# Layer 2's narrow outputs in runs of plain fp32 products, and two layers taking turns by steps

## The chip, the cores and the metric

One NeuronCore of a Trainium2 chip runs the whole kernel. The metric is device time in microseconds (us) of one execution, lower being better. TensorE (PE; its weight loads have rows of their own, PEld) does the matrix products, ScalarE (ACT) and VectorE (DVE) the elementwise work, GpSimd (POOL) a little at the start, and SyncE (SP) issues the DMAs.

## The reference

A causal convolution with seven softmax taps per head runs over (2, 4096, 192) tokens, and its output goes through two gated layers, each 192 → 2048 → 192:

```
x = einsum('hk,bskhg->bshg', softmax(weight), x_unf)     # 8192 tokens x 192
h = x @ w_in1                                            # 192 -> 2048
g = where(h >= 1, h, where(h <= -1, 0, (h + 1)**2 / 4))
x = g @ w_out1                                           # 2048 -> 192
h = x @ w_in2
g = h / (1 + exp(-1.702 * h))
out = g @ w_out2
```

All inputs and outputs are fp32.

## The kernel before

Tokens lie along the free axis, in 16 blocks of 512. The 192 channels are 128 ("a") and 64 ("b"); each layer's 2048 hidden channels are 16 units of 128. A **phase** is one layer of one block. A **step** takes two units: PE makes the hidden values of units u and u+1 in two PSUM banks (`pair`; there are two such pairs, used in turn), ACT and DVE turn them into gated values `a`, and two steps later (`LAG` = 4 units) PE multiplies these by the second weights into two accumulator banks: `acc_a` for the first 128 outputs and `acc_b` for the last 64. There are 256 steps, 8 in a phase. From step 32 on the phases of layer 1 and layer 2 follow one another, 8 whole steps each: layer 1 of block i, then layer 2 of block i-1.

To keep fp32 accuracy in the rounded type fp32r, every operand is split into a high and a low part (`ghi`, `glo` for the gated values, `wh`, `wl` for weights), and three of the four partial products are made. For the 64 narrow outputs the high and low weights lie side by side as 128 columns (`wb`), multiplied by `ghi` and by `glo`: two products, whose two halves of 64 rows of `acc_b` are added when the phase ends.

A product with 128 contraction rows is cut into two of 64 rows, one on the lower and one on the upper half of the PE array, and `couples` (L437) issues them in turn, lower, upper, lower, upper: a **couple** is two such products side by side, usually for different banks. A step (`both`, L468) is 19 couples: 9 for the hidden values, 6 for `acc_a`, 4 for `acc_b`. When a bank has to be written by the other half than the last time, `couples` puts a pause before that product, in which PE's queue waits for a product that carries a signal (a set of numbers, `{6, 18, 37}`, says which of the step's 38 products do).

The gate of layer 1 (`gates`, L368) is: ACT `early` on both banks (L347), ACT `square` on each (L352), DVE `bound` on each (L356, which still reads the hidden bank), ACT `high` (L360) and DVE `low` (L364) on each. Layer 2 needs ACT `early` (L349), `high` and DVE `low` on each bank. So a pair of banks is free for PE once both `bound`s (layer 1) or both `early`s (layer 2) are done. `finish` turns the accumulators into layer 2's input or the output. The convolution's taps (L192, DVE) for coming blocks are spread over the steps by `conv_at`. In the first two steps (`first_only`, L458) hidden values alone are made, in three stretches with a pause ahead of the last; before them the first block's convolution runs on PE in plain fp32 (`conv_by_quarters`, L238, and `conv_by_sides`, L227: 128 rows by 64 columns, two such products side by side in the array's two column halves, three on each side).

Of the kernel before, what the change touches and what calls it, by code (L numbers as in the profile page):

```python
# [10 lines left out]
U32 = mybir.dt.uint32  # L11
# [9 lines left out]
def kernel(  # L21
# [37 lines left out]
    stage = ctx.enter_context(tc.tile_pool(name="stage", bufs=2))  # L59
    xt_p = ctx.enter_context(tc.tile_pool(name="xt", bufs=2))  # L60
    cv_p = ctx.enter_context(tc.tile_pool(name="cv", bufs=2))
    xs_p = ctx.enter_context(tc.tile_pool(name="xs", bufs=4))
    a_p = ctx.enter_context(tc.tile_pool(name="a", bufs=2))
    g_p = ctx.enter_context(tc.tile_pool(name="g", bufs=LAG))
    o_p = ctx.enter_context(tc.tile_pool(name="o", bufs=1))
    ps = ctx.enter_context(tc.tile_pool(name="ps", bufs=1, space=bass.MemoryType.PSUM))
# [43 lines left out]
    words = {1: w1, 2: w2}  # L110
    wt = {n: wpool.tile([P, NG, 2 * WC], F32R, name=f"wt{n}") for n in (1, 2)}
    halves_of = (slice(0, IN), slice(IN, WC))
    whole = slice(0, WC)

    def weight_tile():
        return stage.tile([P, WC, 2], U32, tag="raw", name="raw", bufs=3)

# [13 lines left out]
    def weight_tiles():  # L131
        a = stage.tile([P, WC], F32, tag="wa", name="wa", bufs=2)
        d = stage.tile([P, WC], U32, tag="wd", name="wd", bufs=3)
        return a, d

# [41 lines left out]

    def new_xs():
        return [xs_p.tile([P, T], F32R, tag=t, name=t) for t in ("xah", "xal", "xbh", "xbl")]

    def x_load(part, i, queue=None):

        t = xt_p.tile([P, T + 128], F32, tag=f"xt{part}", name="xt", bufs=2 - part)[:, 0 : PAD + T]
        (queue or nc.sync).dma_start(t, (xb if part else xa)[i])  # L184
        return t
# [89 lines left out]

    def conv_ops(j):

        ta, tb = xt[0, B * j], xt[1, j]
        ca = cv_p.tile([P, T], F32, tag="cva", name="cva")
        cb = cv_p.tile([P, T], F32, tag="cvb", name="cvb", bufs=1)  # L280
        x1[B * j] = new_xs()
        ops = conv_taps(0, ta, ca) + [lambda: put_a(B * j, ca)]
        ops += conv_taps(1, tb, cb) + [lambda: put_b(B * j, cb)]
        st = {}

        def begin():
            st["c"] = cv_p.tile([P, T], F32, tag="cva", name="cva")
            x1[B * j + 1] = new_xs()
            st["ops"] = conv_taps(0, xt[0, B * j + 1], st["c"])
            put_b(B * j + 1, cb)  # L290

        ops.append(begin)
        ops += [lambda: st["ops"].pop(0)() for _ in range(K)] + [lambda: put_a(B * j + 1, st["c"])]
        return ops


    phases = [(1, 0), (1, 1), (2, 0), (2, 1), (1, 2)]
    for i in range(3, NBLK):
        phases += [(1, i), (2, i - 1)]
# [11 lines left out]
    units += in_turn((2, 8), (3, 8), (2, 8), (3, 8))  # L311
    units += [(p, f) for p in range(4, len(phases)) for f in range(NF)]
    unit_at = {u: k for k, u in enumerate(units)}

    hid, act, halves, accs = {}, {}, {}, {}
    HID = 4
# [22 lines left out]
    def gate_ops(u):  # L339

        n, _ = phases[units[u][0]]
        h = hid.pop(u)
        a = a_p.tile([P, 2, T], F32, tag="a", name="a")

        def early(k=slice(0, 2)):
            if n == 1:
                nc.scalar.activation(a[:, k], h[:, k], AF.Relu, bias=0.5, scale=0.5)  # L347
            else:
                nc.scalar.activation(a[:, k], h[:, k], AF.Gelu_apprx_sigmoid)  # L349

        def square(k=slice(0, 2)):
            nc.scalar.activation(a[:, k], a[:, k], AF.Square)  # L352

        def bound(k):
            if n == 1:
                nc.vector.scalar_tensor_tensor(a[:, k], h[:, k], 1.0, a[:, k], op0=ALU.max, op1=ALU.min)  # L356

        def high(k):
            halves[u + k] = [g_p.tile([P, T], F32R, tag=t, name=t) for t in ("ghi", "glo")]
            nc.scalar.copy(halves[u + k][0], a[:, k])  # L360

        def low(k):
            hi, lo = halves[u + k]
            nc.vector.tensor_sub(lo, a[:, k], f32(hi))  # L364

        return early, square, bound, high, low

    def gates(u, conversions=()):  # L368
# [20 lines left out]
        else:  # L389
# [18 lines left out]

    def gemm2_whole(us):

        p = units[us[0]][0]
        acc_a, acc_b = accs[p]
        a, b = [], []
        for u in us:
            wh, wl, wb = out_w(u)
            hi, lo = halves.pop(u)
            a += [(acc_a, wl, hi), (acc_a, wh, hi), (acc_a, wh, lo)]
            b += [(acc_b, wb, hi), (acc_b, wb, lo)]
        closing = (b[-1], a[-1]) if us[-1] == len(units) - 1 else ()
        for x in b + a:  # L420
            nc.tensor.matmul(*x, start=False, stop=any(x is y for y in closing))  # L421

# [45 lines left out]
    def both(u, v):  # L468
# [16 lines left out]
        couples(low, up, banks, fresh, closing, {6, 18, 37})  # L485

    def finish_ops(p):
        i = phases[p][1]
        acc_a, acc_b = accs.pop(p)
        ah, al, bh, bl = x2[i] = new_xs()  # L490
        s = cv_p.tile([P, T], F32, tag="cva", name="s")
        other = slice(DB, P), slice(0, DB)
        return [
            lambda: nc.scalar.copy(s[other[1]], acc_b[other[0]]),
            lambda: nc.scalar.copy(s[other[0]], acc_b[other[1]]),
            lambda: nc.vector.tensor_add(s, acc_b, s),
            lambda: nc.scalar.copy(bh, s),
            lambda: nc.vector.tensor_sub(bl, s, f32(bh)),
            lambda: nc.scalar.copy(ah, acc_a),
            lambda: nc.vector.tensor_sub(al, acc_a, f32(ah)),  # L500
        ]

    def finish(p, step):
# [10 lines left out]
        else:  # L514
            acc_a, acc_b = accs.pop(p)
            o = o_p.tile([P, 2, T + 32], F32, tag="o", name="o")[:, :, 0:T]
            nc.scalar.copy(o[0:DB, 1], acc_b[DB:P])
# [6 lines left out]

            if p < len(phases) - 1:
                at(step + 2, rest)
            else:
                nc.vector.tensor_add(o[0:DB, 1], acc_b[0:DB], o[0:DB, 1])
# [47 lines left out]
    def conv_at(j):  # L576
        first, second = (unit_at[phases.index((1, B * j + k)), 0] for k in range(B))
        ops, begin = [], first - (20 if j == 1 else 22)
        at(begin - 8, lambda: fetch_x((0, B * j), (1, j), (0, B * j + 1)))
        at(begin, lambda: ops.extend(conv_ops(j)))  # L580
        for k in range(2 * (K + 1)):
            at(begin + k, lambda: ops.pop(0)())
        for k in range(K + 2):
            at(second - 16 + k, lambda: ops.pop(0)())

    with tc.manual_schedule():
        first, second = halves_of
        nc.sync.dma_start(taps, taps_in)  # L588
        fetch_x((0, 0), (1, 0))
        pair_x = o_p.tile([P, 2, T + 32], F32, tag="o", name="xt")[:, :, 0 : PAD + T]  # L590
        load_twice(pair_x, xa[1].rearrange("(j p) c -> j p c", j=2))
# [15 lines left out]
        for i in range(B):  # L607
            x1[i] = new_xs()
        ca = cv_p.tile([P, T], F32, tag="cva", name="cva")
        a0 = conv_taps(0, xt[0, 0], ca, exps)  # L610
        db = a_p.tile([P, 2, T], F32, tag="a", name="diag").rearrange("p k t -> p (k t)")
# [3 lines left out]
        da = [f32(t).rearrange("p (k c) -> p k c", c=H) for t in new_xs()[0:2]]  # L615
        da = [[d[:, m] for m in range(K // 2)] for d in da]
# [26 lines left out]
        for j in range(1, NBLK // B):  # L643
            conv_at(j)

        def of(ops, step):
# [30 lines left out]
        beside(1)  # L677
        for u in range(LAG, len(units) + LAG + 4, 2):
            v, step = u - LAG, u // 2
            if u < len(units):  # L680
                both(u, v)
# [5 lines left out]
            elif v < len(units):  # L687
                gemm2_whole((v, v + 1))
            beside(step)
            finish_if_last(v + 1, u + 1)  # L690

# [54 lines left out]
```

## Time and profile before

| | |
|---|---|
| median of 3 runs | 1125.14 us (1124.90 to 1125.28) |
| the profiled execution | 1124.4 us |
| its span, first to last instruction | 1122.6 us |
| PE busy | 1117.6 us, 100% |
| ACT busy | 830.1 us, 74% |
| DVE busy | 709.8 us, 63% |
| granted TensorE clock, mean | 1.00 |

The span is 1.8 us shorter than the profiled execution's time, and the median is 0.74 us above that. Busy time is a union over an engine's instructions. A matmul's row lasts 387 ns on average, but its successors on the same half start 227 ns apart, so times between starts, and not durations, tell what PE is doing.

### The profile page before, as it was taken

The page shows a single profiled execution, that of the slowest core. Times are in us where ns is not written, and L with a number is a line of the kernel's source. Part 1 is how long each engine was busy: PE and PEld are TensorE (multiplying, and loading weights), DVE is VectorE, ACT ScalarE, POOL GpSimd, SP SyncE. Part 2 cuts the span into 40 slices and gives each one's busy share as a digit, 9 for nine tenths or more (in the row PEclk, how much of TensorE's full clock was granted, in tenths as well). Part 3 has the DMA queues.
Part 4 walks back from the last instruction along what each step waited for, and adds up shares of the span by engine and source line. Part 5 has one row for each costly group of instructions (what it writes and reads, how often), then busy time and mean ns, then how long its engine had stood idle before and what let it go on. Part 6 is the DMA issues. An engine that isn't in the chain of part 4 may idle for free.

```text
span 1122.6 us, 23931 instructions
## 1 busy us (share of the span) xinstructions
PE 1117.6 (100%) x9788; PEld 1093.4 (97%) x9788; DVE 709.8 (63%) x1098; ACT 830.1 (74%) x1312; POOL 5.5 (0%) x14
## 2 busy tenths in 40 slices
PE   9999999999999999999999999999999999999998
PEld 5889999999999999999999999999999999999998
DVE  8997767765647557475665755657566575655432
ACT  8998678867767687776877768677686776867754
POOL 1000000000000000000000000000000000000000
PEclk9999999999999999999999999999999999999999
DMA  7442011000100001000010000100001000000000
GB/s 200 136 117 68 1 44 34 1 11 15 30 11 15 11 15 39 10 7 10 16 39 15 1 11 16 39 15 1 11 15 39 15 1 11 15 11 15 1 1 29
DMA packets 23900, 30.71 MB, mean 27 GB/s; under 512 B 3312, under 2 KB 15856, under 8 KB 23792
## 3 DMA queue, kind: packets, MB, share of 16 engines
q1 hardware_dynamic: 23648, 29.06, 9.2%
q8 instruction: 77, 1.26, 0.5%
q14 instruction: 31, 0.25, 0.1%
q10 hardware_dynamic: 144, 0.13, 0.0%
HBM read 19.22 MB, written 6.29 MB: 23 GB/s over the span
## 4 chain that ended last, share of the span: by engine, by line
PE 99%; DMA 0%; SPq 0%; ACT 0%; issue 0%
PE acc L446 51%; PE pair L446 47%; PE cb_ps L238 1%; PE acc L421 0%; DMA xt<-in_xb_dram 0%; PE ca_ps L227 0%; SPq L184 0%; SPq L588 0%; ACT o L531 0%; ACT o L533 0%
## 5 line engine op out<-in xcount | busy, mean ns | idle before, releaser
L446 PE MATMUL acc<-ghi,wt 64*128 64x512 f32 x3048 | 657.6, 387 | 0.0
L446 PE MATMUL acc<-glo,wt 64*128 64x512 f32 x2032 | 566.0, 387 | 0.0
L446 PEld LDWEIGHTS acc<-ghi,wt 64*128 64x128 f32 x3048 | 484.7, 184 | 3.5
L364 DVE TENSOR_TENSOR glo<-a,ghi 128x512 fp32r<-128x512 f32 x512 | 342.7, 690 | 224.5 <-ACT ghi L360 206.7
L446 PE MATMUL pair<-xah,wt 64*128 64x512 f32 x2048 | 429.8, 387 | 0.1
L360 ACT CAST ghi<-a 128x512 fp32r<-128x512 f32 x512 | 314.7, 622 | 44.2 <-DVE a L356 35.3
L446 PEld LDWEIGHTS acc<-glo,wt 64*128 64x128 f32 x2032 | 336.2, 184 | 3.5 <-DVE glo L364 1.0
L446 PE MATMUL pair<-xal,wt 64*128 64x512 f32 x1024 | 308.3, 387 | 0.0
L446 PEld LDWEIGHTS pair<-xah,wt 64*128 64x128 f32 x2048 | 302.5, 185 | 5.0 <-ACT xbh L251 1.6
L356 DVE SCALAR_TENSOR_TENSOR a<-pair,a 128x512 f32<-128x512 f32 x256 | 164.8, 685 | 162.9 <-ACT a L352 142.5
L349 ACT ACTIVATE a<-pair 128x512 f32<-128x512 f32 x256 | 152.2, 595 | 146.4 <-PE pair L446 146.4
L446 PE MATMUL pair<-xbh,wt 64*128 64x512 f32 x1024 | 260.3, 387 | 0.0
L446 PE MATMUL pair<-xbl,wt 64*128 64x512 f32 x512 | 197.2, 387 | 0.0
L446 PEld LDWEIGHTS pair<-xbh,wt 64*128 64x128 f32 x1024 | 186.3, 185 | 1.4
L347 ACT ACTIVATE a<-pair 128x1024 f32<-128x1024 f32 x128 | 131.4, 1026 | 63.7 <-PE pair L446 49.3
L446 PEld LDWEIGHTS pair<-xal,wt 64*128 64x128 f32 x1024 | 153.3, 184 | 1.6 <-DVE xal L254 0.2
L352 ACT ACTIVATE a<-a 128x512 f32<-128x512 f32 (+1 forms) x242 | 146.5, 650 | 4.1
L446 PEld LDWEIGHTS pair<-xbl,wt 64*128 64x128 f32 x512 | 94.1, 184 | 0.7
L192 DVE SCALAR_TENSOR_TENSOR cva<-xt,taps,cva 128x512 f32<-128x512 f32 x84 | 62.9, 749 | 1.5
L192 DVE SCALAR_TENSOR_TENSOR cvb<-xt,taps,cvb 128x512 f32<-128x512 f32 x42 | 31.5, 749 | 0.7
L79 ACT CAST xbh<-cvb 64x512 fp32r<-64x512 f32 x14 | 8.7, 618 | 10.1 <-DVE cvb L192 10.0
L155 DVE SCALAR_TENSOR_TENSOR wd<-wa,wd 128x768 uint32<-128x768 uint32 (+2 forms) x18 | 15.6, 866 | 0.7
(68 smaller groups left out, 249.3 us busy)
## 6 DMA issues: line engine op xcount, KB each, us to landing
raw<-in_w_dram SPq DMA_DIRECT2D x48, 128.0 KB, 2.3
xt<-in_xa_dram SPq DMA_DIRECT2D x17, 259.0 KB, 2.9
out_dram<-o SPq DMA_DIRECT2D x15, 256.0 KB, 2.0
raw<-in_w_dram SPq DMA_DIRECT2D x48, 64.0 KB, 2.3
raw<-in_w_dram SPq DMA_DIRECT2D x16, 192.0 KB, 2.5
out_dram<-o SPq DMA_DIRECT2D x17, 128.0 KB, 2.3
xt<-in_xb_dram SPq DMA_DIRECT2D x8, 259.0 KB, 3.0
xbh<-xbh SPq DMA_DIRECT2D x14, 128.0 KB, 2.2
```

The source lines that it names most:

```text
L79: nc.scalar.copy(hi, src)
L155: nc.vector.scalar_tensor_tensor(d(), a().bitcast(U32), 3, d(), op0=ALU.logical_shift_left, op1=ALU.bitwise_or)
L192: return lambda: nc.vector.scalar_tensor_tensor(c, x, w, c, op0=ALU.mult, op1=ALU.add)
L238: nc.tensor.matmul(c[o], d[k][r, r], t[r, k : k + T], start=k == 0, stop=k == K - 1)
L347: nc.scalar.activation(a[:, k], h[:, k], AF.Relu, bias=0.5, scale=0.5)
L349: nc.scalar.activation(a[:, k], h[:, k], AF.Gelu_apprx_sigmoid)
L352: nc.scalar.activation(a[:, k], a[:, k], AF.Square)
L356: nc.vector.scalar_tensor_tensor(a[:, k], h[:, k], 1.0, a[:, k], op0=ALU.max, op1=ALU.min)
L360: nc.scalar.copy(halves[u + k][0], a[:, k])
L364: nc.vector.tensor_sub(lo, a[:, k], f32(hi))
L446: mm = nc.tensor.matmul(banks[n], w, r, start=n in fresh, stop=ends.get(n) == k)
```

## The change

From step 56 (unit 112; `START`) on, 16 steps form a **superstep** of two phases: layer 1 of block i takes the steps k = 0, 1, 2, 4, 6, 8, 10, 12 (`FIRST`) and layer 2 of block i-1 the steps 3, 5, 7, 9, 11, 13, 14, 15. There are 12 supersteps, and 8 steps of layer 2 alone at the end. Six more things go with it:

- From step 51 (`WIDER`) on, the second products come three steps after the hidden values instead of two. Step 51 itself is a `first_only`.
- From step 59 on a step is `hidden_and_a`: 15 couples, without the 4 for `acc_b`. The order of the two halves alternates with the step's parity. Only the first step of a layer-1 phase (its products fall in k = 3) is still a `both` with 19.
- The narrow outputs are made at the end of a superstep by `exact_b`: plain fp32 products of 128 rows by 64 columns, even and odd units in the two column halves, 14 for layer 1 (its first two units are done by the `both`) and 16 for layer 2, in one run. The weights are high plus low part, added up once by four DVE additions (`join_some`). The gated values stay in SBUF until then, in a ring of 15 slots (`slot`).
- `later_gates` gates layer 1's two banks in the order (1, 0) in even steps and (0, 1) in odd ones.
- `finish` of both phases comes with the run of fp32 products; the convolution of the next block lies beside the layer-1 steps, in slots that are free then (`conv_beside`: two taps in odd steps k from 3 to 11, one in even ones), and takes the 64 channels once for each block instead of once for two.
- At the very end the last three steps' `acc_a` products run whole (`whole_a`), after the last fp32 run.

All SBUF buffers are rearranged so that the slots share room with the weight conversion of the beginning. Up to step 50 each engine's instructions come in the order of before.

```diff
+    EARLY = 7
+    WIDER = 51
...
+    START = len(units) // 2
+    FIRST = (0, 1, 2, 4, 6, 8, 10, 12)
+    for p in range(EARLY, len(phases) - 1, 2):
+        left = {p: list(range(0, NF, 2)), p + 1: list(range(0, NF, 2))}
+        for k in range(NF):
+            q = p if k in FIRST else p + 1
+            f = left[q].pop(0)
+            units += [(q, f), (q, f + 1)]
+    units += [(len(phases) - 1, f) for f in range(NF)]
...
+    def later_gates(u):
+        early, square, bound, high, low = gate_ops(u)
+        if phases[units[u][0]][0] == 1:
+            order = (1, 0) if (u // 2 - START) % 2 == 0 else (0, 1)
+            early()
+            for op in (square, bound, high, low):
+                for k in order:
+                    op(k)
+        else:
+            for k in (0, 1):
+                early(k)
+                high(k)
+                low(k)
...
+    def exact_b(p):
+
+        acc_b = accs[p][1]
+        n = phases[p][0]
+        for f in range(2 if n == 1 else 0, NF):
+            u = unit_at[p, f]
+            w = exact[n][:, f - 2 if n == 1 else f]
+            c = acc_b[f % 2 * DB : f % 2 * DB + DB]
+            nc.tensor.matmul(c, w, made[u // 2][:, f % 2], start=n == 2 and f < 2, stop=f >= NF - 2)
...
+    def hidden_and_a(u, v):
+
+        (low0, up0, b0), (low1, up1, b1) = gemm1_pieces(u), gemm1_pieces(u + 1)
+        low_a, up_a = a_pieces((v, v + 1))
+        if (u // 2 - START) % 2 == 0:
+            low, up, signal = low1 + low0 + b0 + low_a, up_a + up1 + b1 + up0, {4, 11, 16}
+        else:
+            low, up, signal = low_a + low0 + b0 + low1, up0 + up1 + b1 + up_a, {5, 10, 17}
...
+        for u in range(LAG, len(units), 2):
+            step = u // 2
+            v = u - (LAG if step < WIDER else LAG + 2)
+            if step == WIDER:
+                straight, crossed, last, closing = first_only(u)
+                run(straight, last, lambda: crossed(closing))
+            else:
+                (both if v < 2 * START or units[v][1] == 0 and phases[units[v][0]][0] == 1 else hidden_and_a)(u, v)
...
+            if step >= START and (step - START) % NF == NF - 1:
+                p = EARLY + (step - START) // NF * 2
+                exact_b(p)
+                up, down, add, bh, bl, ah, al = finish_ops(p)
+                run(ah, al, up, down, add, bh, bl)
+                exact_b(p + 1)
+                finish(p + 1, 2 * (step + 4))
+        exact_b(len(phases) - 1)
+        for v in range(len(units) - LAG - 2, len(units), 2):
+            whole_a((v, v + 1), v == len(units) - 2)
```

Three places show how instructions move. The first is PE's queue where one step ends and the next begins. Before, two `both` steps (`acc_16_7868` is an `acc_a`, `acc_16_7869` its `acc_b`, `pair_8144` the next step's hidden banks):

```order
L446 MATMUL acc_16_7868<-ghi,wt_93 128x512
L446 MATMUL acc_16_7869<-ghi,wt_93 128x512
L446 MATMUL acc_16_7868<-glo,wt_93 128x512
L446 MATMUL acc_16_7869<-glo,wt_93 128x512
L446 MATMUL pair_8144<-xah,wt_93 128x512 [waits Activation_49]
L446 MATMUL pair_8144<-xah,wt_93 128x512 x3
L446 MATMUL pair_8144<-xal,wt_93 128x512 x2
L446 MATMUL acc_16_7869<-ghi,wt_93 128x512 [waits PE_49]
L446 MATMUL acc_16_7868<-ghi,wt_93 128x512
```

Of the change, the `both` of k = 3 and the `hidden_and_a` of k = 4 (`acc_9_4111` is an `acc_a`, `set_95` layer 1's input):

```order
L545 MATMUL acc_9_4111<-ghi_93,wt_74 128x512
L545 MATMUL acc_9_4112<-ghi_93,wt_74 128x512
L545 MATMUL acc_9_4111<-glo_94,wt_74 128x512
L545 MATMUL acc_9_4112<-glo_94,wt_74 128x512
L545 MATMUL pair_4164<-set_95,wt_74 128x512 [waits DVE_49]
L545 MATMUL acc_9_4111<-ghi_87,wt_74 128x512 [waits PE_49]
L545 MATMUL pair_4164<-set_95,wt_74 128x512
L545 MATMUL acc_9_4111<-ghi_87,wt_74 128x512
L545 MATMUL pair_4164<-set_95,wt_74 128x512
```

The wait for PE's own signal, ahead of the first product that takes an accumulator to the other half, stood three couples into the step (six `pair` rows and a pair of accumulator rows are three to four couples); it now stands at the step's second product.

The second place is PE's queue around a superstep's end. Before there is only the junction shown above. Of the change, the last couple of k = 15, the run of fp32 products for layer 1 (`acc_7`) and layer 2 (`acc_8`), and the next superstep's first couple (a row marked x4 is four products that read alike; `slots` are the kept gated values):

```order
L545 MATMUL pair_3900<-set_1231,wt_75 128x512
L545 MATMUL acc_7_3379<-glo_86,wt_74 128x512
L520 MATMUL acc_7_3380<-slots_3259,exact_b 64x512 x4
L520 MATMUL acc_7_3380<-slots_3422,exact_b 64x512 x2
...
L520 MATMUL acc_8_3520<-slots_3853,exact_b 64x512 [waits Activation_49] x2
L520 MATMUL acc_8_3520<-slots_3259,exact_b 64x512 [waits Activation_49] x2
L545 MATMUL pair_3980<-set_95,wt_74 128x512
L545 MATMUL acc_8_3519<-ghi_91,wt_75 128x512
```

Between the couples there are now 30 products of another shape, in which PE asks nothing of the newest step's gates until the last four.

The third place is ACT's queue. Before, within a layer-1 phase and into layer 2 (`pair_4018` and `pair_4074` are hidden banks):

```order
L347 ACTIVATE a<-pair_4018 128x1024 [waits PE_49]
L352 ACTIVATE a<-a 128x512 [waits Activation_49]
L352 ACTIVATE a<-a 128x512
L360 CAST ghi<-a 128x512 [waits DVE_49,PE_49] x2
L349 ACTIVATE a<-pair_4074 128x512 [waits PE_49]
L360 CAST ghi<-a 128x512 [waits PE_49,Activation_49]
```

Of the change, steps k = 0 and 1 of a superstep and the start of k = 2 (`pair_3980`, `pair_4023`, `pair_4068`), behind the copy out of the last narrow accumulator:

```order
L643 COPY slots_3769<-acc_8_3520 64x512 [waits PE_49]
L416 ACTIVATE slots_3259<-pair_3980 128x1024 [waits PE_49]
L421 ACTIVATE slots_3259<-slots_3259 128x512 [waits Activation_49]
L421 ACTIVATE slots_3259<-slots_3259 128x512
L430 CAST ghi_93<-slots_3259 128x512 [waits DVE_49]
L430 CAST ghi_91<-slots_3259 128x512 [waits DVE_49]
L416 ACTIVATE slots_3259<-pair_4023 128x1024 [waits PE_49]
L421 ACTIVATE slots_3259<-slots_3259 128x512 [waits Activation_49]
L421 ACTIVATE slots_3259<-slots_3259 128x512
L430 CAST ghi_87<-slots_3259 128x512 [waits DVE_49]
L430 CAST ghi_89<-slots_3259 128x512 [waits DVE_49]
L416 ACTIVATE slots_3259<-pair_4068 128x1024 [waits PE_49]
```

The instructions of one layer-1 step are the same five; what moved is that three such steps now stand behind one another while a step of PE has 15 couples instead of 19, and that later ones alternate with layer 2.

## Rows read from the trace of the kernel before

**Rows 1.** The page: the chain that ended last, by engine.

```profile
PE 99%; DMA 0%; SPq 0%; ACT 0%; issue 0%
```

**Rows 2.** Windows: stretch, us, busy (count) of PE, PEld, DVE, ACT, POOL, clock, DMA.

```profile
500.00:1100.00 600.00, 600.00 (x5298) 600.00 (x5296) 353.67 (x537) 431.99 (x690) 0.00 (x0) 1.00 0.05 15
```

**Rows 3.** Timeline of PE: start us, us, what; first products of two steps.

```profile
601.21 0.66 PE L446 MATMUL pair<-xah,wt 64*128 64x512 f32 x4
...
1109.39 0.66 PE L446 MATMUL pair<-xah,wt 64*128 64x512 f32 x4
```

**Rows 4.** Groups by line and form: plain fp32 products of one side (three in code).

```profile
L227 PE MATMUL ca_ps<-xt,xah 128*64 128x512 f32 x6 | 3.0, 608 | 0.0
```

**Rows 5.** Timeline of weight loads: fp32 by quarters, one row for each pass.

```profile
5.79 0.18 PEld L238 LDWEIGHTS cb_ps<-xt,diag 64*64 64x64 f32 x4 [0.25 <-issue]
...
10.08 0.18 PEld L238 LDWEIGHTS cb_ps<-xt,diag 64*64 64x64 f32 x4 [0.25 <-issue]
```

**Rows 6.** Timeline of PE: a pause, then couples, fp32 sides, and couples again.

```profile
13.37 0.39 PE L446 MATMUL pair<-xbl,wt 64*128 64x512 f32 x2
...
13.82 0.30 PEld L446 LDWEIGHTS pair<-xah,wt 64*128 64x128 f32 x4 [0.49 <-PE pair L446]
...
14.16 0.19 PEld L446 LDWEIGHTS pair<-xal,wt 64*128 64x128 f32 x2
...
14.39 0.40 PE L446 MATMUL pair<-xal,wt 64*128 64x512 f32 x2
...
14.71 0.64 PE L227 MATMUL ca_ps<-xt,xah 128*64 128x512 f32 x1
...
15.19 0.59 PE L227 MATMUL ca_ps<-xt,xah 128*64 128x512 f32 x1
...
15.19 0.14 PEld L227 LDWEIGHTS ca_ps<-xt,xah 128*64 128x64 f32 x1 [0.29 <-issue]
...
16.05 0.59 PE L227 MATMUL ca_ps<-xt,xah 128*64 128x512 f32 x1
...
16.58 0.73 PE L446 MATMUL pair<-xah,wt 64*128 64x512 f32 x4
...
16.92 0.19 PEld L446 LDWEIGHTS pair<-xal,wt 64*128 64x128 f32 x2
```

**Rows 7.** Timeline: the gates of a layer-1 step and a layer-2 step.

```profile
561.32 0.39 PE L446 MATMUL pair<-xbl,wt 64*128 64x512 f32 x1
...
561.80 1.03 ACT L347 ACTIVATE a<-pair 128x1024 f32<-128x1024 f32 x1 [0.58 <-PE pair L446]
...
563.52 1.29 DVE L356 SCALAR_TENSOR_TENSOR a<-pair,a 128x512 f32<-128x512 f32 x2 [1.58 <-ACT a L352]
...
564.30 1.23 ACT L360 CAST ghi<-a 128x512 fp32r<-128x512 f32 x2 [0.29 <-DVE a L356]
...
564.96 1.29 DVE L364 TENSOR_TENSOR glo<-a,ghi 128x512 fp32r<-128x512 f32 x2
...
566.74 0.62 ACT L360 CAST ghi<-a 128x512 fp32r<-128x512 f32 x1
...
567.26 0.59 ACT L349 ACTIVATE a<-pair 128x512 f32<-128x512 f32 x1
```

**Rows 8.** Timeline: a weight load that waited for VectorE.

```profile
18.73 0.74 DVE L254 SCALAR_TENSOR_TENSOR xal<-ca_ps,share,xah 128x512 fp32r<-128x512 f32 x1
...
19.53 0.19 PEld L446 LDWEIGHTS pair<-xal,wt 64*128 64x128 f32 x2 [0.23 <-DVE xal L254]
```

**Rows 9.** Groups by line and form: the convolution's taps on VectorE.

```profile
L192 DVE SCALAR_TENSOR_TENSOR cva<-xt,taps,cva 128x512 f32<-128x512 f32 x84 | 62.9, 749 | 1.5
```

**Rows 10.** Timeline of PE: from the last couples to whole products.

```profile
1113.47 0.44 PE L446 MATMUL acc<-glo,wt 64*128 64x512 f32 x2
...
1113.84 0.50 PE L421 MATMUL acc<-ghi,wt 128*128 128x512 f32 x1
...
1114.18 0.40 PE L421 MATMUL acc<-glo,wt 128*128 128x512 f32 x1
```

More of the change, by code (lines that the diff above doesn't have):

```diff
@@ L111, with room @@
     wt = {n: wpool.tile([P, NG, 2 * WC], F32R, name=f"wt{n}") for n in (1, 2)}
+    SLOTS = NF - 1
+    def room(tag, count, kind=F32):
+        return big.tile([P, count], kind, tag=tag, name=tag)
+    raw_room, words_room, made_room = (room(f"slots{k}", 3 * 2 * T) for k in (0, 3, 6))
+    pair_room, a_room = (room(f"slots{k}", 2 * 2 * T) for k in (9, 11))
+    early_set = room("slots13", 2 * 2 * T, F32R)
+    diag_room = room("set0", 4 * T)
+    g_tiles = [[room(f"{t}{k}", T, F32R) for t in ("ghi", "glo")] for k in range(6)]
@@ new lines, with slot @@
+    set1 = room("set1", 4 * T, F32R)
+    conv_room = room("exact_b", (2 * NF - 2) * DB)
+    s_room = room("s", T)
+    begins = {0: 3, 3: 3, 6: 3, 9: 2, 11: 2, 13: 2}
+    slots = {}
+    def slot(k):
+        k %= SLOTS
+        if k not in slots:
+            first = max(b for b in begins if b <= k)
+            t = room(f"slots{first}", begins[first] * 2 * T).rearrange("p (s k t) -> p s k t", k=2, t=T)
+            slots.update({first + j: t[:, j] for j in range(begins[first])})
+        return slots[k]
@@ new lines, with set_of @@
+    o_early = pair_room[:, 0 : 2 * T + 64].rearrange("p (k t) -> p k t", k=2)
+    conv_a, conv_b = conv_room[:, 0:T], conv_room[:, T : 2 * T]
+    xts = {0: in_turns([made_room[:, 3 * WC :], pair_room[:, 9 * P :]]), 1: in_turns([conv_room[:, 2 * T :]])}
+    a_early = in_turns([a_room[:, k * 2 * T : (k + 1) * 2 * T].rearrange("p (k t) -> p k t", k=2) for k in (0, 1)])
+    def set_of(t):
+        return [t[:, k * T : (k + 1) * T] for k in range(4)]
+    sets = {"early": set_of(early_set), "halves": g_tiles[4] + g_tiles[5], "one": set_of(set1)}
@@ L112, with input_set @@
+    def input_set(which):
+        if which == "zero" and "zero" not in sets:
+            sets["zero"] = set_of(room("set0", 4 * T, F32R))
+        return sets[which]
+    set_of_x1 = {0: "early", 1: "halves", 2: "early", 3: "zero", 4: "early"}
+    set_of_x2 = {0: "one", 1: "zero", 2: "one"}
+    exact = {}
     halves_of = (slice(0, IN), slice(IN, WC))
@@ L176, with new_x1, new_x2, x_load @@
     x1, x2 = {}, {}
[L178 to L184, printed above, removed]
+    def new_x1(i):
+        x1[i] = input_set(set_of_x1.get(i, "one"))
+    def new_x2(i):
+        x2[i] = input_set(set_of_x2.get(i, "zero"))
+        return x2[i]
+    def x_load(part, i, where=None):
+        t = (xts[part]() if where is None else where)[:, 0 : PAD + T]
+        nc.sync.dma_start(t, (xb if part else xa)[i])
         return t
@@ L311 @@
     units += in_turn((2, 8), (3, 8), (2, 8), (3, 8))
-    units += [(p, f) for p in range(4, len(phases)) for f in range(NF)]
+    units += [(p, f) for p in range(4, EARLY) for f in range(NF)]
+    START = len(units) // 2
[7 more added lines that the diff above has]
+    units += [(len(phases) - 1, f) for f in range(NF)]
     unit_at = {u: k for k, u in enumerate(units)}
-    hid, act, halves, accs = {}, {}, {}, {}
+    hid, made, halves, accs = {}, {}, {}, {}
     HID = 4
@@ L358, in high @@
         def high(k):
-            halves[u + k] = [g_p.tile([P, T], F32R, tag=t, name=t) for t in ("ghi", "glo")]
+            at = u % 4 if step < WIDER else (4, 2, 0)[(step - WIDER) % 3]
+            halves[u + k] = g_tiles[at + k]
             nc.scalar.copy(halves[u + k][0], a[:, k])
@@ L485, in both, with a_pieces, pieces @@
         couples(low, up, banks, fresh, closing, {6, 18, 37})
+    def a_pieces(us):
+        acc_a = acc_banks(units[us[0]][0])[0]
+        parts = [(*out_w(u)[:2], *halves.pop(u)) for u in us]
+        def pieces(r):
+            return [(acc_a, w[r], g[r]) for wh, wl, hi, lo in parts for w, g in ((wl, hi), (wh, hi), (wh, lo))]
+        return pieces(slice(0, H)), pieces(slice(H, P))
+    def hidden_and_a(u, v):
[5 more added lines that the diff above has]
+            low, up, signal = low_a + low0 + b0 + low1, up0 + up1 + b1 + up_a, {5, 10, 17}
+        p, f = units[v]
+        if f == 0:
+            acc_tiles(p)
+        acc = acc_banks(p)[0]
+        banks = hidden_banks(u) | {acc: accs[p][0]}
+        hidden = {HID + u % 4, HID + (u + 1) % 4}
+        fresh = hidden | ({acc} if f == 0 else set())
+        couples(low, up, banks, fresh, hidden | ({acc} if units[v + 1][1] == NF - 1 else set()), signal)
     def finish_ops(p):
         i = phases[p][1]
-        acc_a, acc_b = accs.pop(p)
-        ah, al, bh, bl = x2[i] = new_xs()
-        s = cv_p.tile([P, T], F32, tag="cva", name="s")
+        acc_a, acc_b = accs[p]
+        ah, al, bh, bl = new_x2(i)
+        s = s_room
         other = slice(DB, P), slice(0, DB)
```

157 lines of the change are left out of this document (99 added, 58 removed).

## The prediction

> **What bounds the kernel now.** I read the chain that ended last first: 99% of it is PE [rows 1]. The windows say the same of the long middle: in 600 us PE is never idle, at full clock (1.00), with DVE busy for 354 and ACT for 432 of them [rows 2]. So ACT and DVE have slack, and the time is the number of PE's products times their spacing, as long as nobody is late. The spacing comes from the timeline: between two equal places that are 118 steps apart lie 508.18 us [rows 3], which is 4.307 us a step and, with 19 couples in it, 0.2267 us a couple (118 is the whole number that fits: 5298 products in 600 us are 139.4 steps of 38, or 4.30 us). A whole product at the end has the same spacing.
>
> **The change, part by part.**
>
> *Couples removed.* Before there are 254 steps of 19 couples, 18 couples in the first two steps and 20 whole products at the end: 4864 slots. After: 49 steps of 19 up to step 50, 9 couples in step 51, 7 steps of 19 (52 to 58), then 185 of 15 and 12 of 19, the 18 of the beginning and 18 whole products: 4112. That is 752 slots fewer, at 0.2267: −170.5 us.
>
> *fp32 products added.* 12 runs of 30 and a last one of 16 make 376 products, two side by side: 188 pairs. What a pair costs is the question of this change. The kernel has the same shape in the first block's convolution: three fp32 products on each side are six records [rows 4], so each is two passes. The passes on one side start at 15.19 and, two later, at 16.05: 0.43 us each, with the other side's beside them [rows 6]. The longer run by quarters has its loads at 5.79 and, ten passes later, at 10.08: 0.429 us [rows 5]. 376 passes at 0.429: +161.3 us. The net is −9.15 us, 5% of what is exchanged: for every two units two passes of 0.429 (0.858) replace four couples of 0.2267 (0.907).
>
> *A rule that says otherwise.* In [rows 6] the load for the next pass begins at 15.19, together with the pass ahead of it, takes 0.14 us and delays nothing, although both use all 128 rows. The Trainium skill, "TensorE: Matmul & The Clock Gate", Part 3 (What overlaps and what doesn't), says that loads overlap with running matmuls only when their row groups differ; here they don't. By that the 376 passes would each pay the load, 53 us in all. The rows of this case contradict it, over a short run of passes.
>
> *Changing shape.* [Rows 6] have one change in and one out. Into fp32: 14.39 to 14.71 is 0.32 where a couple takes 0.23, and 14.71 to 15.19 is 0.48 where a pass takes 0.43: +0.14. Out: 16.05 to 16.58 is 0.53 for 0.43, and 16.58 to the second couple at 16.92 is 0.34 for 0.23: +0.21. So 0.35 for each of 13 runs: +4.55. The last run also takes the place of the change from couples to whole products, which costs 1113.47 to 1113.84 and on to 1114.18 [rows 10], 0.37 + 0.34 − 2 × 0.23 = 0.25: −0.25.
>
> *The pause that moved.* In a `both` the lower half writes `acc_a` last; the `hidden_and_a` behind it (k = 4) opens with the upper half on `acc_a`. The order shows the wait at its second product, and the signal waited for is the last product of the step before. `first_only` has this very case: 13.37 to 13.82, 0.45 for 0.23, then 0.34 for 0.23 to the next couple at 14.16 [rows 6]: +0.33, or 0.22 if the second part is hidden. Behind this wait PE's whole queue stands. Here one lower product goes ahead of it, so I take 0.30, 12 times: +3.6. Step 51, a `first_only`, adds 0.33 once. The other pauses keep their distance of about four couples, at which rows of before show no gap.
>
> *Three layer-1 steps behind one another.* A step is now 15 × 0.2267 = 3.40 us. In [rows 7] ACT starts `early` 0.48 after the last hidden product's start (561.32 to 561.80), so 0.25 after the next step begins; the second `bound` ends 3.01 after that (563.52 + 1.29 − 561.80), and ACT's last cast at 3.73 (565.53). The next `early` may start 0.10 before that cast ends, as 567.26 does before 566.74 + 0.62. So with three layer-1 steps in a row ACT needs 3.63 to 3.73 for a step of 3.40. Count from the end of k = 0: its `early` starts at 0.25, that of k = 1 at 3.88 to 3.98, and the second `bound` of k = 1 ends at 6.89 to 6.99. The `both` of k = 3 wants that bank with its very first product, at 2 × 3.40 = 6.80. A load starts 0.06 after VectorE's end (19.47 to 19.53) [rows 8], so it is 0.15 to 0.25 late, and a restart costs the 0.11 seen above: 0.26 to 0.36. I take 0.31. The first superstep is exempt, since its steps k = 0 to 2 are still `both`s of 4.31 us: 11 times, +3.4. What is late after that: nothing, as the `both` of k = 3 gives ACT 4.31 us.
>
> *Hidden work.* Extra taps (7 more for every second block), four additions of weights and five more loads of the input lie beside PE: DVE idles for 246 of 600 us [rows 2]. If that cover went, a tap costs 0.75 us [rows 9]. `finish` runs under 12.9 us of fp32 products, and its result is wanted three steps later. The last fp32 run covers the last gates. The tail behind the last product is unchanged, and so, in order, is everything before step 51; I allow 0.5 us either way for its rearranged buffers.
>
> *The sum.* −9.15 + 4.55 − 0.25 + 3.6 + 0.33 + 3.4 = +2.5 us. On the profiled execution's 1124.4 us (span 1122.6) that is 1126.9 (1125.1); the median shown is 0.74 above that execution, so 1127.6. Bounds: 0.22 to 0.33 for the pause (−1.0, +0.4), 0 to 0.6 for the bank (−3.4, +3.2), 0.30 to 0.40 for the shapes (±0.65), 0.428 to 0.430 for a pass (±0.4).
>
> **Rivals.**
>
> *PE's queue takes both waits ahead of time (faster).* The queue may reach the waiting products of k = 3 and k = 4 while earlier ones still run, so that waiting costs the array nothing: −9.15 + 4.55 − 0.25 + 0.33 = −4.5, 1120.6. For it: the couples of before carry three such waits a step and show no gap. Against: those stand four couples behind their signal, and where the signal is the product just before, [rows 6] show the gap. It decides at 0.38 us of waits in a superstep (4.5 / 12); I count about 0.6.
>
> *One of the two waits is absent.* For instance because the bank comes free 0.25 us earlier, or the pause hides in the half that runs ahead: −1.1 to −0.9, about 1124.1, no change.
>
> *VectorE falls behind (slower still).* In the steps 4 to 11 two steps of PE (6.80 us) hold two `bound`s and two `low`s (2 × 1.29 [rows 7]), two more `low`s (1.4) and three taps (2.25 [rows 9]): 6.2 us, 92%, where the middle of before has 59%. VectorE works in order, and two taps stand ahead of the next layer-1 step's first `bound`. A bank has about 0.7 us to spare there, which speaks against it. Each 0.5 us a superstep adds 6 us: 1133.6.
>
> *fp32 passes don't overlap.* With loads exposed, 0.14 × 376 = 53 us more: 1180. With the column halves one after the other, 161 us more: 1289. [Rows 6] show both hidden, in runs of four passes; the new runs have thirty.
>
> **How the numbers follow.** The forecast gets 0.48, no new waits 0.16, one wait 0.16, VectorE behind 0.18, loads exposed 0.01, halves one after the other 0.01. Predicted: 1127.6; alone it would range from 1125.8 to 1129.4. For 8 in 10 the range reaches half into the cases on both sides: 1121 to 1132. About 0.2%, 2.25 us, is what a measurement of this kernel can tell from no change, so 1122.9 to 1127.4 is the same. The forecast lies astride the upper end: 0.27 of its 0.48 are slower. Slower 0.27 + 0.18 + 0.02 = 0.47, same 0.21 + 0.16 = 0.37, faster 0.16.
>
> **What would show it.** Passes in the fp32 runs 0.429 us apart, loads hidden; a run and its two changes 13.2 us long; in every superstep but the first a weight load at k = 3 that waits for `bound` (L425), some 0.3 us; at k = 4 a wait of PE for PE of the same size; otherwise 0.2267 us a couple. It is wrong if a pass is not 0.429 (0.005 are 1.9 us), if the waits are absent or longer, or if PE idles in steps 5 to 15.

## The result, and the profile after

| | before | changed |
|---|---|---|
| median | 1125.02 us (1124.61 to 1125.28, 4 runs) | 1134.17 us (1133.10 to 1134.54, 4 runs) |
| the profiled execution, its span | 1124.4, 1122.6 | 1134.37, 1132.6 |
| DVE, ACT busy | 709.8, 830.1 | 732.4, 820.7 |

The ratio is 1.0080 (95% interval 1.0063 to 1.0098): slower, by 9.2 us. Forecast were +2.5 us and a range up to 1132, so the direction is right, and the time is 2 us outside the range.

The page of the changed kernel, its span and the chain that ended last (by engine), answers to [rows 1]; PE is no longer alone on the chain:

```profile
span 1132.6 us, 21706 instructions
...
PE 97%; DMA 1%; ACT 1%; SPq 0%; issue 0%; DVE 0%; DVEq 0%
```

Windows of the changed kernel (columns as in [rows 2]; a number in brackets counts instructions):

```profile
0.00:30.00 30.00, 29.00 (x204) 16.10 (x206) 24.13 (x47) 25.01 (x44) 6.20 (x14) 1.00 0.74 205
30.00:40.00 10.00, 5.57 (x42) 4.37 (x40) 4.98 (x9) 4.59 (x6) 0.00 (x0) 0.87 0.19 49
40.00:60.00 20.00, 20.00 (x176) 18.69 (x174) 19.06 (x32) 18.33 (x24) 0.00 (x0) 0.98 0.43 119
60.00:230.00 170.00, 170.00 (x1504) 164.12 (x1502) 131.73 (x208) 138.50 (x212) 0.00 (x0) 1.00 0.16 46
...
37.00:41.00 4.00, 3.34 (x16) 2.90 (x18) 3.78 (x8) 3.97 (x6) 0.00 (x0) 0.57 0.00 0
...
500.00:1100.00 600.00, 600.00 (x4738) 446.45 (x4736) 370.84 (x568) 424.57 (x688) 0.00 (x0) 1.00 0.06 16
```

The last line answers to [rows 2]: in the supersteps PE is as full as before, and DVE gained only 17 us in 600. The second one is the news. The same ten microseconds of the kernel before:

```profile
30.00:40.00 10.00, 10.00 (x90) 8.27 (x88) 9.60 (x17) 9.21 (x12) 0.00 (x0) 1.00 0.52 144
```

There are 48 products fewer there now, 24 couples or 5.4 us, and the granted clock falls: 0.57 from 37 to 41 us. That is long before step 51. Product by product (counted from 0), the changed kernel is 0.55 us behind at number 200 (29.67 against 29.13 us), 6.75 at number 300 (47.21 against 40.46), and 6.59 from number 1000 to step 51. Of the 10.0 us between the two profiled spans 6.6 lie where I had written "unchanged in order". The timeline there:

```profile
26.27 0.89 ACT L202 ACTIVATE slots<-slots 128x768 f32<-128x768 f32 x1
...
32.84 0.39 PE L545 MATMUL acc<-glo,wt 64*128 64x512 f32 x2
34.76 0.56 DVE L205 TENSOR_SCALAR slots<-slots 128x768 uint32<-128x768 uint32 x1 [5.07 <-DMA slots<-in_w_dram]
35.36 0.96 DVE L208 SCALAR_TENSOR_TENSOR slots<-slots,slots 128x768 uint32<-128x768 uint32 x1
36.23 1.28 DVE L425 SCALAR_TENSOR_TENSOR slots<-pair,slots 128x512 f32<-128x512 f32 x2
36.35 0.83 ACT L214 CAST wt<-slots 128x768 fp32r<-128x768 f32 x1 [5.37 <-DVE slots L208]
...
37.63 0.53 PEld L545 LDWEIGHTS pair<-ghi,wt 64*128 64x128 f32 x4 [4.82 <-ACT wt L214]
37.66 1.22 PE L545 MATMUL pair<-ghi,wt 64*128 64x512 f32 x4 [4.43 <-DVE slots L425]
...
38.65 0.66 PE L545 MATMUL pair<-glo,wt 64*128 64x512 f32 x2
...
39.08 0.66 PE L545 MATMUL acc<-ghi,wt 64*128 64x512 f32 x2
...
41.06 0.39 PE L545 MATMUL pair<-ghi,wt 64*128 64x512 f32 x1
```

Read it from the bottom up. PE starts at 37.66, when two things that it needs are there: its weights, whose cast (L214) ends at 37.18, and a hidden bank, whose second `bound` (L425) ends at 37.51; so the `bound` is what PE waited for last. The cast waited for VectorE's join (L208), and the two `bound`s stand behind that join in VectorE's queue; the join waited for the shift (L205), and the shift for a DMA, 5.07 us. Afterwards couples come 0.43 us apart (38.65, 39.08), as at the lower of the two clock levels (1.2 GHz), until 41 us.

Which DMA is it? The weights arrive as 64-bit numbers (the description ahead called all inputs fp32), a high and a low 32-bit word each: `scale` (L202, ACT) reads the high words, `shift` (DVE) the low ones. In step 3 the program issues the loads of weight tile (1, 6) and then the shift of tile (1, 3). Before, each tile is a buffer of its own from a pool of three, and the load, though issued first, waits until (1, 3) is done with. In the change both are views of one room. There the order of the program counts: the load waits only for what was issued ahead of it, the `scale` that ends at 27.16; it runs, and the shift, issued behind it, waits for its end, and takes (1, 6)'s low words for (1, 3)'s last three bits: beside the time, a small error in these weights. The shift and the load's DMAs of the kernel before, and behind them the load's DMAs of the changed kernel:

```profile
29.15 0.55 DVE L152 TENSOR_SCALAR wd<-raw 128x768 uint32<-128x768 uint32 x1
...
29.77 4.64 SPq L129 DMA_DIRECT2D raw<-in_w_dram  x7
```

```profile
27.19 3.54 SPq L184 DMA_DIRECT2D slots<-in_w_dram  x7
```

No instruction had moved; what one of them waits for had changed.

In the supersteps, the timeline around a run of fp32 products, and around k = 3 and k = 4 of the superstep behind it:

```profile
315.37 0.39 PE L545 MATMUL acc<-glo,wt 64*128 64x512 f32 x1
...
315.69 1.94 PE L520 MATMUL acc<-slots,exact_b 128*64 128x512 f32 x8
316.17 0.14 PEld L520 LDWEIGHTS acc<-slots,exact_b 128*64 128x64 f32 x2 [0.29 <-issue]
316.60 0.14 PEld L520 LDWEIGHTS acc<-slots,exact_b 128*64 128x64 f32 x2 [0.29 <-issue]
...
328.18 0.60 PE L520 MATMUL acc<-slots,exact_b 128*64 128x512 f32 x2
328.71 0.50 PE L545 MATMUL pair<-set,wt 64*128 64x512 f32 x1
...
329.05 0.39 PE L545 MATMUL pair<-set,wt 64*128 64x512 f32 x1
...
332.45 1.03 ACT L416 ACTIVATE slots<-pair 128x1024 f32<-128x1024 f32 x1 [3.02 <-PE pair L545]
...
336.03 1.02 ACT L416 ACTIVATE slots<-pair 128x1024 f32<-128x1024 f32 x1
...
338.86 0.39 PE L545 MATMUL acc<-glo,wt 64*128 64x512 f32 x1
...
339.08 0.53 PEld L545 LDWEIGHTS pair<-set,wt 64*128 64x128 f32 x6 [0.26 <-DVE slots L425]
...
343.30 0.39 PE L545 MATMUL acc<-glo,wt 64*128 64x512 f32 x2
...
343.75 0.18 PEld L545 LDWEIGHTS acc<-ghi,wt 64*128 64x128 f32 x1 [0.26 <-PE acc L545]
343.75 0.50 PE L545 MATMUL acc<-ghi,wt 64*128 64x512 f32 x1
...
344.09 0.39 PE L545 MATMUL acc<-ghi,wt 64*128 64x512 f32 x1
```

Passes are 0.43 us apart and their loads lie beside them, as in [rows 6]. Into the run: 315.37 to 315.69 is 0.32 for 0.23, and the first pass takes 0.48 for 0.43. Out of it: 0.53 (328.18 to 328.71) for 0.43, and 0.34 (328.71 to 329.05) for 0.23. At k = 4 the upper half goes from 343.30 to 343.75 and on to 344.09. From run to run a superstep takes 69.23 us (mean of 11); the forecast's terms add up to 69.15.

### The profile page after: what moved, and what is told of

The parts are those of the page before. It is cut to its first block, busy times and chain, and to the rows that moved or that the text cites. A ratio compares the mean times of both kernels' runs of the same rounds, so it can differ in the third digit from the quotient of the medians.

```text
span 1132.6 us, 21706 instructions
## 1 busy us (share of the span) xinstructions
PE 1123.5 (99%) x9038; PEld 878.0 (78%) x9038; DVE 732.4 (65%) x1137; ACT 820.7 (72%) x1312; POOL 6.2 (1%) x14
## 4 chain that ended last, share of the span: by engine, by line
PE 97%; DMA 1%; ACT 1%; SPq 0%; issue 0%; DVE 0%; DVEq 0%
PE pair L545 47%; PE acc L545 35%; PE acc L520 14%; DMA slots<-in_w_dram 1%; PE cb_ps L295 1%; PE acc L500 0%; SPq L184 0%; PE ca_ps L258 0%; ACT slots L202 0%; ACT slots L421 0%; DVE slots L425 0%; ACT ghi L308 0%; ACT slots L416 0%; ACT slots L308 0%; DVE slots L208 0%
## 5 line engine op out<-in xcount | busy, mean ns | idle before, releaser
L545 PE MATMUL pair<-set,wt 64*128 64x512 f32 x4032 | 748.6, 388 | 0.1
L545 PEld LDWEIGHTS pair<-set,wt 64*128 64x128 f32 x4032 | 593.4, 184 | 75.3 <-issue 9.7
L545 PE MATMUL acc<-glo,wt 64*128 64x512 f32 x1284 | 441.6, 387 | 0.0
L434 DVE TENSOR_TENSOR glo<-slots,ghi 128x512 fp32r<-128x512 f32 x512 | 342.2, 690 | 130.5 <-ACT ghi L430 106.6
L430 ACT CAST ghi<-slots 128x512 fp32r<-128x512 f32 x512 | 314.4, 621 | 38.1 <-DVE slots L425 29.7
L425 DVE SCALAR_TENSOR_TENSOR slots<-pair,slots 128x512 f32<-128x512 f32 x256 | 164.8, 685 | 139.9 <-ACT slots L421 139.5
L416 ACT ACTIVATE slots<-pair 128x1024 f32<-128x1024 f32 x128 | 131.4, 1027 | 100.6 <-PE pair L545 99.7
L418 ACT ACTIVATE slots<-pair 128x512 f32<-128x512 f32 x256 | 152.0, 594 | 40.7 <-PE pair L545 25.3
L520 PE MATMUL acc<-slots,exact_b 128*64 128x512 f32 x752 | 164.2, 594 | 0.0
L421 ACT ACTIVATE slots<-slots 128x512 f32<-128x512 f32 (+1 forms) x242 | 146.4, 649 | 4.1
```

What stands on the lines that cost most here:

```text
L520: nc.tensor.matmul(c, w, made[u // 2][:, f % 2], start=n == 2 and f < 2, stop=f >= NF - 2)
L545: mm = nc.tensor.matmul(banks[n], w, r, start=n in fresh, stop=ends.get(n) == k)
```

## The experiments

Every time is a median of 4 to 11 runs, beside 1124.8 us for the kernel before on the same chip (1125.07 for the last run). A superstep's length is the mean distance of the starts of fp32 runs in the trace.

**1. The shift ahead of the load.** On the changed kernel:

```diff
-                run(*of(fetches, step), *of(dve, step))
+                run(*of(dve, step), *of(fetches, step))
```

> One line of the changed kernel is turned round: in a step VectorE's part of the weight conversion is issued ahead of the weight loads, not behind them. Theory A: the 6.6 us that the changed kernel is behind at 60 us come from one place. The load of weight tile (1, 6) stands ahead of the shift of tile (1, 3) and goes into the same room, so the shift waits for the end of that load (34.5 us), the join, the cast and PE wait behind it, and PE runs at the lower clock for a while after it. Turned round, the load waits for the shift, as before the change; the stall of 4.8 us and the slow couples behind it are gone, about 6.0 us: 1128.2 us, 1.003 of the kernel before. Rival: the shared rooms as such are what delays the conversion (loads that land late, buffers that come free late); then the order of these two changes nothing, 1134, or the stall moves to another tile and half of it stays, 1131.

Measured: 1127.23 us (1126.66 to 1127.78), ratio 1.0022 (1.0013 to 1.0031); 6.9 us less than the changed kernel. Of this run, the same window:

```profile
30.00:40.00 10.00, 10.00 (x92) 8.27 (x90) 9.60 (x17) 9.20 (x12) 0.00 (x0) 1.00 0.52 142
```

and the timeline of the same conversion, shift, join and cast of tile (1, 3):

```profile
29.12 0.56 DVE L205 TENSOR_SCALAR slots<-slots 128x768 uint32<-128x768 uint32 x1
...
29.71 0.96 DVE L208 SCALAR_TENSOR_TENSOR slots<-slots,slots 128x768 uint32<-128x768 uint32 x1
...
30.70 0.84 ACT L214 CAST wt<-slots 128x768 fp32r<-128x768 f32 x1 [0.20 <-DVE slots L208]
```

PE is full again, the clock does not fall, and at 200 us the trace is level with that of before (0.04 us). The shared rooms as such cost nothing. The 0.9 us beyond the expected 6.0 contain the 0.55 that the changed kernel was behind before the stall and that this execution was not. Those need not come from the change: the start varies from execution to execution, and in the eleven traces product 200 starts anywhere from 28.66 to 30.11 us, in the kernel of experiment 3 at 29.59. In the traces the supersteps, too, are 0.06 us shorter here (69.17 us).

**2. The same order, another room.** The loads stay ahead, and tile (1, 6) alone is loaded into the room of the diagonals, idle then:

```diff
-    raws = in_turns([words_of(r[:, k * 2 * WC : (k + 1) * 2 * WC]) for r, k in ((raw_room, 0), (raw_room, 1), (words_room, 0))])
+    raws = in_turns([words_of(r[:, k * 2 * WC : (k + 1) * 2 * WC]) for r, k in ((raw_room, 0), (raw_room, 1), (words_room, 0)) * 2 + ((diag_room, 0), (raw_room, 1), (words_room, 0)) + ((raw_room, 0), (raw_room, 1), (words_room, 0)) * 3])
```

> The changed kernel, with the loads ahead of VectorE's part as there, but weight tile (1, 6) alone goes into a room that nothing else uses at that time. Theory A (the shift of tile (1, 3) waits because the load goes into its own room): the stall is gone as in the first run, 1127.2 us, and the load of (1, 6) no longer waits for anything. Rival (it is the order of the loads and VectorE's work as such, or SyncE's queue, which stands behind this load): the stall stays, 1134.

Measured: 1127.82 us (1126.77 to 1129.46), ratio 1.0027 (1.0018 to 1.0037). The shift of tile (1, 3) in this run:

```profile
28.67 0.55 DVE L205 TENSOR_SCALAR slots<-slots 128x768 uint32<-128x768 uint32 x1
```

The stall is gone with the order kept, so neither the order nor SyncE's queue was its cause, but the room in common.

**3. The kernel before, turned round** by the same line as in experiment 1.

> The kernel before, with the one line turned round (VectorE's part ahead of the weight loads). Theory A: there each weight tile has a buffer of its own from a pool of three, the load waits for the shift in either order, and nothing changes: 1124.8 us. Rival: the order costs something in every kernel of this kind, and the kernel before gets faster by 0.5 to 6 us.

Measured: 1124.88 us, ratio 1.0000 (0.9992 to 1.0009). As theory A says.

**4. The other half at k = 3.** On experiment 1, in `both`:

```diff
-        low = low1 + low_b + low0 + b0 + low_a
-        up = up0 + up_a + up1 + b1 + up_b
+        if v < 2 * START:
+            low, up, signal = low1 + low_b + low0 + b0 + low_a, up0 + up_a + up1 + b1 + up_b, {6, 18, 37}
+        else:
+            low, up, signal = low1 + low_a + low0 + b0 + low_b, up0 + up_b + up1 + b1 + up_a, {6, 18, 37}
```

> As the run before, and in the twelve steps k = 3 the two accumulators change places: the 128 wide outputs end on the upper half, on which k = 4 begins them, and the 64 narrow ones on the lower. Theory A: the wait of PE for its own product at the second product of k = 4 is gone, and with it the later wait of one half at k = 6, which comes from the half that ran ahead at the pause: 0.33 x 12 = 3.9 us less than the run before, 1124.3 us. Rival: what k = 4 waits for is mostly covered by what comes at k = 6; then PE only reaches the bank of k = 6 earlier and waits there, and 0.13 x 12 = 1.6 us are won, 1126.6.

Measured: 1122.66 us (1122.06 to 1124.09), ratio 0.9984 (0.9975 to 0.9993). PE's twelve waits at k = 4 are gone, and with them the long distances between products at k = 6; a superstep takes 68.86 instead of 69.17 us: 0.31 x 12 = 3.7 us, as theory A says. The medians are 4.6 apart, the profiled spans 3.6; the rival's 1.6 is below all of these.

**5. The hidden banks apart.** On experiment 1; `one` are four single banks, which replace the two pairs from step 56 on:

```diff
...
+        return [None] + [hidden_room[1].tile([P, T], F32, tag=f"one{2 * k + j}", name=f"one{2 * k + j}") for j in (0, 1)]
...
-            early()
-            for op in (square, bound, high, low):
+            for k in order:
+                early(k)
+                square(k)
+                bound(k)
+            for op in (high, low):
                 for k in order:
                     op(k)
...
```

> As the first run, and from step 56 on the two hidden banks of a step are tiles of their own, with a gate of their own each: ScalarE's first instruction of a layer-1 gate is two of 512 instead of one of 1024, and the gate goes bank by bank. Before, PE's first product into the pair waits for the second bound, whichever bank it writes. Theory A: couples of 231 to 236 ns, about 0.17 us a superstep, come from banks that come free just in time; they go, 2.0 us less, but the second bound now ends 0.1 to 0.2 later, and k = 3 wants both banks at once, so its wait grows from 0.11 to about 0.25: +1.5. In sum 1127.7 us, 0.5 less than the first run. Rival: ScalarE, which gets 0.17 us more for each layer-1 step, falls behind in the three layer-1 steps in a row and k = 3 waits 0.5 or more: +4 us, 1130 or above.

Measured: 1126.64 us (1126.43 to 1127.01), ratio 1.0017 (1.0007 to 1.0026). The sum came as expected (0.6 us less than experiment 1, for 0.5), its parts did not, so that is luck. The wait at k = 3 did not grow, it went: each bank's gate begins when that bank is done, which I had not counted. A superstep takes 69.01 instead of 69.17 us, 1.8 us over twelve. Against that stands a wait of 1.2 us that I had not seen coming, once, at the hand-over of the banks (in experiment 6 it shows best).

**6. All three,** with this order at k = 3 (the lower half's bank first, the other four couples later), and gates in the order (1, 0) at k = 1:

```diff
...
+            low, up, signal = low1 + low_a + low_b + low0 + b0, up_b + up0 + up1 + b1 + up_a, {6, 10, 18, 37}
...
```

> The three edits together, and at k = 3 the lower bank alone is wanted by the first couple, the other one four couples later, with the gate of k = 1 in that order. Theory A: no wait is left in the supersteps but the two changes of shape: against the second run 0.11 x 11 for k = 3 and 0.17 x 12 for the couples, 3.2 us less: 1121.1 us, 0.9965 of the kernel before. Rival: the couples of 231 to 236 ns have another cause (the couples of 15 a step as such), and 1.2 us alone are won: 1123.1; or ScalarE falls behind, and it is slower than the second run.

Measured: 1121.47 us (1121.10 to 1122.43), ratio 0.9972 (0.9962 to 0.9982). A superstep is 68.57 us, 0.29 less than in experiment 4, or 3.4 us over twelve, as theory A says. But 1.2 alone arrived, the rival's sum, though not for its reason. 1.2 went to the hand-over; this run's timeline at step 56, where the first product into a single bank waits for the last read of the pair that goes:

```profile
252.63 0.62 ACT L438 CAST ghi<-slots 128x512 fp32r<-128x512 f32 x1
252.65 0.53 PEld L557 LDWEIGHTS one<-slots,wt 64*128 64x128 f32 x6 [1.36 <-ACT slots L426]
252.65 0.73 PE L557 MATMUL one<-slots,wt 64*128 64x512 f32 x4 [0.93 <-ACT slots L426]
```

The rest, 1.0, lies ahead of the supersteps, nearly all of it between 19 and 22 us of this execution, whose instructions there are those of experiment 4: the start varies, as above. How much of it the other executions have is not shown.

**7. Handed over one by one:** on experiment 6, each pair in a pool of its own, closed at its own turn.

```diff
...
-        if len(hidden_room) == 1:
-            rooms[0].__exit__(None, None, None)
-            hidden_room.append(ctx.enter_context(rooms[1]))
+        if hidden_room[2 + k] is None:
+            rooms[k].__exit__(None, None, None)
+            hidden_room[2 + k] = ctx.enter_context(rooms[2 + k])
...
```

> As the run with all three edits; there PE waits 1.32 us once, at step 56, because the two pairs of banks are handed over to the four single ones together, when the gates of both are done. Here each pair is handed over by itself, when its own turn comes. Theory: this wait goes, 1.1 us less, about 1120.4 us and 0.996 of the kernel before; the supersteps stay at 68.57 us. Rival: the hand-over waits for the gates of the step before in any case, and nothing changes.

Measured: 1120.42 us (1120.02 to 1120.75), ratio 0.9961 (0.9948 to 0.9973), superstep 68.57. This version beats both kernels.

**8. Two runs for one.** On experiment 4:

```diff
+            if step >= START and (step - START) % NF == NF - 2 and step < len(units) // 2 - 8:
+                exact_b(EARLY + (step - START) // NF * 2)
             if step >= START and (step - START) % NF == NF - 1:
                 p = EARLY + (step - START) // NF * 2
-                exact_b(p)
```

> As the second run (shift ahead, other half at k = 3), but layer 1's fp32 products come behind step k = 14 and only layer 2's behind k = 15: as many products in two runs instead of one, so twelve changes of shape in and twelve out more. Theory: 0.15 in and 0.21 out, 0.36 x 12 = 4.3 us more than the second run, 1127.0 us: the price of a change is that of the term in the sum, wherever it stands. Rival: a part of it belongs to the wait for what stands behind the run (the gates of the newest step), and a run that asks nothing of them costs less: 1124.8.

Measured: 1127.63 us (1127.24 to 1128.30), ratio 1.0026 (1.0016 to 1.0036): 5.0 more than experiment 4 (4.0 by the spans). Of its trace, PE into layer 1's run and out of it:

```profile
305.16 0.39 PE L545 MATMUL acc<-glo,wt 64*128 64x512 f32 x1
...
305.48 1.51 PE L520 MATMUL acc<-slots,exact_b 128*64 128x512 f32 x6
...
311.64 0.49 PE L545 MATMUL acc<-ghi,wt 64*128 64x512 f32 x1
...
311.97 0.39 PE L545 MATMUL acc<-ghi,wt 64*128 64x512 f32 x1
```

0.32 for 0.23 in; 6.16 for 14 passes of 0.429 (6.01); 0.33 for 0.23 out: 0.35, the term of the sum. The 4.2 us for twelve of them lie between the two measures; the rival's 2.1 is below both.

**9. Shorter runs.** On experiment 7, `exact_b` makes only the first two units' products of layer 2 and leaves out the other fourteen; the narrow outputs lack them.

> The run with pairs handed over one by one, with 14 of layer 2's 16 fp32 products left out in each of the 13 runs: its narrow outputs lack these. 13 x 7 pairs of two passes are 182 passes. Theory: a pass is worth its spacing in the trace, 0.429 us, and nothing else hangs on it: 78.1 us less, 1042.3 us. By that two passes (0.858) stand against four couples (0.907) for every two units, and the exchange is worth 0.049 us times 188, 9 us, and no more. Rival: part of a run lies over waits that would come otherwise (the newest gates, the copies out of the accumulators), which a run of half the length no longer hides: 1 us or more a superstep is given back, 1054 or above.

Measured: 1043.12 us (1042.07 to 1043.65), ratio 0.9273 (0.9257 to 0.9288): 77.3 us for 182 passes, 0.425 each (the spans, 1119.0 and 1040.3, give 0.432). A superstep takes 62.55 instead of 68.57 us, 0.430 for each of its 14 passes. A pass is worth its spacing; the runs hide nothing that would come otherwise.

## Why the prediction was right and wrong

| step of the sum | forecast, us | measured, us |
|---|---|---|
| couples for fp32 passes | −9.15 | passes 0.429 apart; 0.425 to 0.432 in experiment 9 |
| changes of shape, and the tail | +4.55 − 0.25 | 0.15 in, 0.21 out, 13 times: +4.7; tail as before |
| pause at k = 4 | +3.6 | 0.33 x 12 = +4.0; 3.7 in experiment 4 |
| step 51 | +0.33 | +0.4 |
| bank at k = 3 | +3.4 | 0.11 x 11 = +1.2 |
| couples that come late by some ns | none | about 0.2 x 12 = +2.4 |
| everything before step 51 | 0, ± 0.5 | +6.6 (the stall 6.2, the start the rest) |
| sum | +2.5 | +9.9 (spans: +10.0) |

**The step that failed** is the last: "unchanged, and so, in order, is everything before step 51; I allow 0.5 us either way for its rearranged buffers". The order was unchanged. A wait was not: the shift of weight tile (1, 3) came to wait for the next load into its room. Experiments 1 to 3 show it from three sides. With it mended, the changed kernel takes 1127.23 us, where 1127.6 was forecast. That it comes so near is in part luck: two terms of the sum were wrong by about as much in opposite directions, the bank at k = 3 by 2.2 us and the late couples by some 2. I had read the order, and not what each instruction waits for, in a stretch in which DVE and ACT have no slack (9.60 and 9.21 of 10 us in the window of before): there one late instruction is at once on the path.

**The exchange of products** is right, and small as forecast. The rule that I had set against the rows (the Trainium skill, "TensorE: Matmul & The Clock Gate", Part 3, What overlaps and what doesn't: a load overlaps only if its row group differs) holds here no more than there: 376 passes of 128 rows hide their loads of 0.14 us, in runs of thirty. The changes of shape cost what [rows 6] showed, 0.15 us in and 0.21 out. The Trainium skill, "TensorEngine Tiling (Array Packing)", Tiling Modes, says that a change of mode drains the engine; that such a change costs time agrees with it.

**The pause at k = 4** came as computed. It has a sequel that I missed: the half that is not held runs one couple ahead, and at k = 6 it is held by its bank until both halves are level (its products start at 350.24, 350.55 and 350.89, 0.31 and 0.34 for 0.23):

```profile
349.21 1.29 DVE L425 SCALAR_TENSOR_TENSOR slots<-pair,slots 128x512 f32<-128x512 f32 x2 [1.75 <-ACT slots L421]
...
350.24 0.39 PE L545 MATMUL pair<-set,wt 64*128 64x512 f32 x1
...
350.55 0.50 PE L545 MATMUL pair<-set,wt 64*128 64x512 f32 x1
...
350.89 0.39 PE L545 MATMUL pair<-set,wt 64*128 64x512 f32 x1
```

Experiment 4 removes both waits.

**The bank at k = 3** was mis-sized. The gates of k = 0 and 1 begin at 332.45 and 336.03, 3.57 apart and not 3.63 to 3.73, and the weight load comes at 339.08, just when the couple is due (338.86 + 0.23). What is lost is only that the load no longer lies beside the couple before: 0.11.

**The late couples** are a term that I had set at nothing ("otherwise 0.2267"). Behind a layer-1 step whose bank comes free just in time, the next couples are 231 to 236 ns apart, five or so each time. Between 315 and 1100 us 973 products come 229 to 250 ns after the one before on their half, none in the same stretch of the kernel before, 685 in experiment 1, 316 in experiment 5 and 175 in experiment 6. That most of them go with separate banks is shown; that late weight loads make them is only argued. The order (1, 0) that `later_gates` gives the banks had no effect by itself, for PE's first product waited for the second `bound`, whichever bank it wrote, until the banks were tiles of their own: at k = 6 the product that writes the bank read first starts at 350.55, behind the second `bound` (349.21 + 1.29), not the first. No run tries the order alone.

Of the rivals, none had the stall. "VectorE falls behind" would have given 1133.6, near what was measured, but for another reason: a number that fits is no proof. In its place (steps 4 to 11) one half of PE does wait for a `bound`, at k = 6, so the sign "PE idles in steps 5 to 15" was met in small; but VectorE had stood idle for 1.75 us ahead of that `bound` (the row at 349.21), so it had not fallen behind.

## What to carry to other kernels

When buffers of a pool become views of one shared tile, the order of the program takes the place of the pool's release, for the time and for what is read: compare every wait, and not only the order, of the instructions that touch them. A stretch where several engines are above 90% deserves this check first, however far it is from the edit. And where a step is held on one half of the array or by one bank of two, letting each wait for its own (another half, another tile) was worth 6.8 us here (1127.23 to 1120.42), more than the 4.7 that the exchange of products brings after its changes of shape.

## What was not expected of the hardware

After 4.4 us without a product PE came back at the lower clock: granted 0.57 between 37 and 41 us, couples 0.43 us apart instead of 0.227, and 1.00 again from 41 us on. Some eight couples at 0.2 us more are 1.6 us, a quarter of what the stall cost.
